# Alphas of the first two groups scanned straight from the PSUM banks, the first group in chunks of 128

## The chip, the cores and the metric

The kernel runs on one core of one Trainium2 chip. The metric is the device time of a run in microseconds (us). A core's engines each work through a queue of their own, in order: TensorE (PE in the profile; PEld its weight loads), VectorE (DVE), ScalarE (ACT), GpSimd (POOL) and SyncE (SP), which here only issues transfers. Engines wait for each other by semaphores. TensorE writes to PSUM, eight banks of 128 partitions by 512 float32 numbers.

## The reference

A gated linear attention, whose output feeds a gated state space block:

```python
# q, k, v, alpha: (4, 8, 768, 48)
for t in range(S):
    state = alpha[:, :, t, :, None] * state + np.einsum('bhd,bhe->bhde', k[:, :, t], v[:, :, t])
    y[:, :, t] = np.einsum('bhd,bhde->bhe', q[:, :, t], state)
x = y.transpose(0, 2, 1, 3).reshape(B, S, H * D)
proj = x @ w_in                      # 384 to 2 * 512
val, gate = proj[..., :512], proj[..., 512:]
for t in range(S):
    h = exp(A_log) * h + val[:, t]
    ys[:, t] = h
out = (gate * sigmoid(gate) * ys) @ w_out
```

## The kernel before

The sequence of each of the four batches is cut into three groups of 256 positions (`GC`), twelve groups in all (`m` = 0 to 11); a group has two chunks `c` of 128 positions. Attention is made chunk by chunk from scores and a carried state. For that the running product of the alphas along the sequence is needed (`prod`), and for the keys its inverse (`inv`): queries are multiplied by `prod`, keys by `inv`, both into `Z`. Two heads lie side by side on the partitions (64 each), four such pairs along the free axis, so a group's alphas are 128 x 1024 numbers.

- `products(m)` (L616) makes `prod` by one scan forwards (L629) and `inv` by one scan backwards (L641), each 1024 long and both on VectorE; small steps set the scans' starting values in `first` and `last` and note a check value in `ratio`.
- The first three groups (`NAT`) are loaded in natural order and turned by TensorE: `natural_alpha` (L572) transposes the alphas into two banks and copies them to `aT` (ScalarE L584, for chunk 1 of group 0 VectorE L586). `natural_qk` (L589) transposes keys or queries into two banks, and its `times(c)` (L603) multiplies them into `Z` on VectorE. Later groups are turned on VectorE (L620).
- `keys(m, c)` (L659) transposes the scaled keys back, ScalarE copies them (L666). `scores` (L668) makes two banks of scores; `masks` (L678) multiplies them by a triangular mask: one bank on VectorE (L687), one by a copy on ScalarE (L685) and a product on GpSimd (L686). For chunk (0, 1) both are made on VectorE (L683).
- `values`, `carried` and `state` (L689, L701, L713) make the output `y` and the state; `join` (L724) copies `y` out and places it in `xT`, partly by small transfers.
- `project`, `hidden`, `gate` and `output` (L747 to L800) are the second block; L755 is its projection, whose weights are converted from float64 bits by `high_word` (VectorE), `low_word` (ScalarE) and `word_sum` (GpSimd).

The order on each engine is the order in the text, from L814 on. First come the loads, all on SP but two on ScalarE's queue: alphas, keys and queries of group 0, alphas of group 1, values 0, keys and queries of group 1, values 1, then the weights. Then `constants` (L473), fillers for TensorE (`warm`, L827 to L831, which multiply the identity and whose result nobody uses), and the transposes. Group 0's `prod` and `inv` are made whole, then its four products into `Z`, then group 1's first scan; scores, masks, values and state of group 0 follow, then group 1's inverse, products, keys, scores and masks. From the first `project` (L907) on TensorE alternates between the two blocks.

PSUM: `ps_sc` has two banks for each of two tags (scores, `y` and, at first, keys and queries), `ps_mm` three, `ps_st` one for the state.

Of the kernel before, what the change touches and what calls it, by code (L numbers as in the profile page):

```python
# [346 lines left out]
def fast(  # L347
# [41 lines left out]
    ps_sc = pool("ps_sc", 2, space=PS)  # L389
    ps_st = pool("ps_st", 1, space=PS)  # L390
    ps_mm = pool("ps_mm", 3, space=PS)
# [76 lines left out]
    invs = inv[:, 1:].rearrange("p (h n) -> p h n", h=4)  # L468
    ratio = const.tile([C, N, 4], FP32, name="ratio")
# [6 lines left out]
    def constants():  # L476
        for m, engine in ((0, nc.vector), (1, nc.gpsimd)):
            if m:
                make_identity(nc, ident)

                nc.gpsimd.memset(mask, 1.0)
                nc.gpsimd.affine_select(out=mask, in_=mask, compare_op=ALU.is_ge, fill=0.0, base=0,
                                        channel_multiplier=-1, pattern=[[1, C]])
                for t in vs:
                    nc.gpsimd.memset(t[:, :, :, D:64], 0.0)

            for name in "akq":
                engine.memset(natural(name, m)[:, :, :, D:64], 1.0)
        for t, x in ((minus, -1.0), (start_p, FIRST_PRODUCT), (aT[:, 4 * GC:], 0.0), (first, FLOOR),
                     (last, 0.0), (one, 1.0)):  # L490
            nc.vector.memset(t, x)
        for m in range(2):
            for name in "akq":
                nc.gpsimd.memset(raw_bufs[m][name].rearrange("p h n -> p (h n)")[:, G * H * 64:], 1.0)
# [77 lines left out]
    def natural_alpha(m, banks=None):  # L572

        tps = []
        for c in range(G):
            tp = (banks or ps_mm).tile([C, 4, C], FP32, tag=f"sc{c}" if banks else "mm", name="tn")
            for p in range(4):
                nc.tensor.transpose(tp[:, p, :], natural("a", m)[:, c, 2 * p:2 * p + 2, :], ident)
            tps.append(tp)

        def evict():
            for c in range(G):
                if m or not c:
                    nc.scalar.activation(alphas[:, :, ds(c * C, C)], tps[c], AF.Copy)  # L584
                else:
                    nc.vector.tensor_copy(out=alphas[:, :, ds(c * C, C)], in_=tps[c])  # L586
        return evict

    def natural_qk(m, name, banks=None):  # L589
# [3 lines left out]
        tps = []  # L593
        for c in range(G):
            tp = (banks or ps_sc).tile([C, 4, C], FP32, tag="mm" if banks else f"sc{c}", name="tn")
            for p in range(4):
                nc.tensor.transpose(tp[:, p, :], natural(name, m)[:, c, 2 * p:2 * p + 2, :], ident)
            tps.append(tp)

        def times(c):  # L600
            i, by = {"k": (1, invs), "q": (0, prods)}[name]
            cols = ds(c * C, C)
            nc.vector.tensor_mul(Zs[m][:, :, i, cols], tps[c], by[:, :, cols])  # L603
# [12 lines left out]
    def products(m):  # L616
# [6 lines left out]
        if m >= NAT:  # L623
            check_alpha(m)
            turn("a", alphas)
        nc.vector.tensor_mul(first[:, :, 0], alphas[:, :, 0], prods[:, :, GC - 1] if g else start_p)
        nc.vector.memset(alphas[:, :, 0:1], 0.0)
        yield
        nc.vector.tensor_tensor_scan(  # L629
            out=prod, data0=aT[:, 0:4 * GC], data1=first.rearrange("p h n -> p (h n)"),  # L630
# [4 lines left out]
        if g:  # L635
            nc.vector.tensor_mul(ratio[:, m], end, inv_end)
        else:
            nc.vector.tensor_scalar(out=ratio[:, m], in0=end, scalar1=1.0 / FIRST_PRODUCT, scalar2=None,
                                    op0=ALU.mult)
        nc.vector.reciprocal(inv_end, end)  # L640
        nc.vector.tensor_tensor_scan(  # L641
            out=inv[:, ::-1], data0=aT[:, ::-1],
# [232 lines left out]
    for _ in steps:  # L875
        pass
# [153 lines left out]
```

## Time and profile before

| what | us |
|---|---|
| median of 4 runs | 296.03 (295.69 to 296.67) |
| the profiled execution | 294.53 |
| its span, from first to last instruction | 292.8 |
| busy: TensorE, VectorE, GpSimd, ScalarE | 283.3, 225.2, 112.4, 99.9 |
| landing of group 0's first alphas (issue 0.81 + 3.8) | 4.6 |
| first scores on TensorE (L675) | 15.01 |
| first projection (L755) | 30.92 |

The mean granted clock of TensorE in the profiled execution was 0.999 of full speed. A line of the timeline has the start (from the span's start), the duration, engine, source line, operation, the tile written and the tiles read, the shape, and how many instructions were merged; in square brackets how long the engine had been idle before and what ended that.

### The profile page before, as it was taken

The numbers are of one execution on the slowest core, as the hardware profiler recorded it, in microseconds if no ns is written. First come the engines' busy times: TensorE is split into PE (matmuls) and PEld (weight loads), VectorE is DVE, ScalarE is ACT, GpSimd is POOL, SyncE is SP. The second block draws the span as 40 slices with busy tenths as digits, with TensorE's granted clock in tenths as the row PEclk, the third lists the DMA queues.
The fourth block names the chain that finished last, engine by engine and source line by source line (L and its number), as shares of the span: only waits on it lengthen the run. The fifth ranks groups of instructions, "written<-read, shape, count | busy, mean of one in ns | idle before, by whom it ended". The sixth has DMA issues, their size and how long they took to land. (4 is left out here: it accounts for less than half of the span.)

```text
span 292.8 us, 6119 instructions
## 1 busy us (share of the span) xinstructions
PE 283.3 (97%) x2343; PEld 225.4 (77%) x2343; DVE 225.2 (77%) x262; ACT 99.9 (34%) x221; POOL 112.4 (38%) x114
## 2 busy tenths in 40 slices
PE   7799999999999999999999999999999999999991
PEld 3488877886886886886886896886886886886870
DVE  5997897999996898898799799799699694312211
ACT  4267534434333332323432431432441531331110
POOL 7017791374712612642612613642513542401110
PEclk9999999999999999999999999999999999999999
DMA  9999979999992991991991891991891401101101
GB/s 129 163 161 305 370 131 173 231 264 215 255 181 76 231 152 51 238 182 49 239 164 44 220 199 29 234 191 34 224 205 33 109 12 35 54 11 31 54 4 63
DMA packets 71230, 42.08 MB, mean 144 GB/s; under 512 B 47492, under 2 KB 70536, under 8 KB 71192
## 3 DMA queue, kind: packets, MB, share of 16 engines
q1 hardware_dynamic: 69760, 40.96, 68.8%
q0 software_dynamic: 384, 0.44, 0.7%
q8 instruction: 20, 0.33, 0.5%
q10 hardware_dynamic: 1048, 0.20, 0.5%
q14 instruction: 18, 0.15, 0.2%
HBM read 33.33 MB, written 4.72 MB: 130 GB/s over the span
## 5 line engine op out<-in xcount | busy, mean ns | idle before, releaser
L771 POOL TENSOR_TENSOR f<-sg,hh 128x256 f32<-128x256 f32 x48 | 60.3, 1257 | 94.7 <-ACT sg L770 44.9
L755 PE MATMUL pv<-xT,w_in 128*128 128x256 f32 x288 | 72.3, 387 | 0.0
L755 PE MATMUL pg<-xT,w_in 128*128 128x256 f32 x288 | 70.3, 380 | 0.0
L785 PE MATMUL o<-w_out,f 128*128 128x384 f32 x192 | 64.0, 486 | 0.0
L755 PEld LDWEIGHTS pg<-xT,w_in 128*128 128x128 f32 x288 | 54.5, 190 | 8.1 <-DVE hh L763 0.8
L755 PEld LDWEIGHTS pv<-xT,w_in 128*128 128x128 f32 x288 | 52.8, 190 | 10.0 <-issue 1.9
L686 POOL TENSOR_TENSOR A<-A,mask 128x512 f32<-128x512 f32 x23 | 28.8, 1271 | 67.8 <-ACT A L685 67.8
L785 PEld LDWEIGHTS o<-w_out,f 128*128 128x128 f32 x192 | 36.4, 190 | 22.6 <-POOL w_out L535 0.3
L770 ACT ACTIVATE sg<-pg 128x256 f32<-128x256 f32 x48 | 18.4, 384 | 93.6 <-PE pg L755 88.9
L763 DVE TENSOR_TENSOR_SCAN hh<-a_dec,hh,pv 128x256 f32<-128x256 f32 x32 | 23.3, 727 | 24.0 <-PE pv L755 24.0
L629 DVE TENSOR_TENSOR_SCAN prod<-aT,first 128x1024 f32<-128x1024 f32 x12 | 33.0, 2748 | 0.1
L687 DVE TENSOR_TENSOR A<-sc,mask 128x512 f32<-128x512 f32 x23 | 15.7, 690 | 20.0 <-PE sc L675 19.8
L641 DVE TENSOR_TENSOR_SCAN inv<-aT,last 128x1025 f32<-128x1025 f32 x12 | 30.0, 2504 | 0.4
L793 ACT ACTIVATE o_sb<-o 128x384 f32<-128x384 f32 x22 | 10.8, 491 | 42.7 <-PE o L785 42.7
L675 PE MATMUL sc<-Z 48*128 48x128 f32 x384 | 24.9, 279 | 0.0
L675 PEld LDWEIGHTS sc<-Z 48*128 48x128 f32 x384 | 22.4, 188 | 2.8 <-issue 1.8
L698 PE MATMUL y<-A,v 128*64 128x128 f32 x384 | 23.7, 274 | 0.2 <-POOL A L686 0.2
L698 PEld LDWEIGHTS y<-A,v 128*64 128x64 f32 x384 | 20.7, 137 | 0.8 <-POOL A L686 0.4
L620 DVE STREAM_TRANSPOSE aT<-raw_a 128x1024 f32<-128x1024 f32 x9 | 18.4, 2040 | 0.0
L620 DVE STREAM_TRANSPOSE Z<-raw_q 128x1024 f32<-128x1024 f32 x9 | 18.2, 2023 | 0.0
L620 DVE STREAM_TRANSPOSE Z<-raw_k 128x1024 f32<-128x1024 f32 x9 | 18.2, 2018 | 0.0
L719 PEld LDWEIGHTS st<-v,ktm 128*64 128x64 f32 x320 | 11.4, 137 | 3.4 <-issue 3.0
(91 smaller groups left out, 264.4 us busy)
## 6 DMA issues: line engine op xcount, KB each, us to landing
raw_k<-in_k_dram SPq DMA_DIRECT2D x24, 192.0 KB, 5.1
raw_q<-in_q_dram SPq DMA_DIRECT2D x24, 192.0 KB, 6.4
v<-in_v_dram SPq DMA_DIRECT2D x24, 192.0 KB, 6.6
out_dram<-o_sb SPq DMA_DIRECT2D x24, 192.0 KB, 1.9
raw_a<-in_alpha_dram SPq DMA_DIRECT2D x23, 192.0 KB, 3.9
raw_a<-in_alpha_dram SPq DMA_DIRECT2D x18, 176.0 KB, 4.0
raw_k<-in_k_dram SPq DMA_DIRECT2D x18, 176.0 KB, 5.9
raw_q<-in_q_dram SPq DMA_DIRECT2D x18, 176.0 KB, 6.9
```

The lines of the kernel that those rows point to most:

```text
L620: nc.vector.transpose(out=to.rearrange("p h (c j) -> p h j c", j=NT), in_=raw_bufs[m % NR][name].rearrange("p h (j d) -> p h j d", d=D)[:, ...
L629: nc.vector.tensor_tensor_scan(out=prod, data0=aT[:, 0:4 * GC], data1=first.rearrange("p h n -> p (h n)"), initial=0.0, op0=ALU.mult, op1= ...
L641: nc.vector.tensor_tensor_scan(out=inv[:, ::-1], data0=aT[:, ::-1], data1=last.rearrange("p h n -> p (h n)")[:, 0:4 * GC + 1][:, ::-1], in ...
L675: nc.tensor.matmul(sc[i][:, p, :], Z[rows, p, 1, cols], Z[rows, p, 0, cols], start=True, stop=True)
L686: nc.gpsimd.tensor_mul(A[:, 1], A[:, 1], mb)
L687: nc.vector.tensor_mul(A[:, 0], sc[0], mb)
L698: nc.tensor.matmul(ys[m][i][ds(64 * s, 64), e, ds(c * C, C)], v_sb[:, c, 2 * p + i, :], A[:, i, p, :], start=(c == 0 and e == 0), stop=Fal ...
L755: nc.tensor.matmul(pj, w_in[cc][:, kk, vg, :], xT[:, kk, :], start=(kk == 0), stop=(kk == NK - 1))
L763: nc.vector.tensor_tensor_scan(out=hh, data0=a_dec[:, cc:cc + 1].to_broadcast([C, GC]), data1=pv, initial=prev_h[cc][:, GC - 1:GC] if n % ...
L770: nc.scalar.activation(sg, pg, AF.Silu)
L771: return lambda: nc.gpsimd.tensor_mul(fs[n][:, cc, :], sg, hhs.pop((n, cc)))
L785: nc.tensor.matmul(os[c], fs[n][:, cc, ds(c * C, C)], w_out[:, cc, :], start=(cc == 0), stop=(cc == NI - 1))
```

## The change

PSUM becomes one pool `ps` with named banks: three for single tiles in turn (`mm`, "b0", "b1", "b6"), and pairs that alternate between "b4"/"b5" and one tile over two adjacent banks ("b23", `both`).

Group 0: alphas stay in their two banks, and `chunk_products` scans each chunk there, 512 at a time, with its own `first_c`, `last_c`, `prod_c` and `inv_c`. The second chunk starts from the end of the first (`ends`). Keys and queries of a chunk are multiplied, and its scores and masks begin, before the next chunk is scanned. Masks are split into `masks_far` (ScalarE and GpSimd) and `masks_near` (VectorE), for chunk (0, 1) as well.

Group 1: alphas are transposed into the two adjacent banks, and `products(1, al)` scans all 1024 from there. Of its four products into `Z`, that of the first chunk's queries is a copy on ScalarE (`q_sb`) and a product on GpSimd. The scores of both chunks stand ahead of its `keys`.

The loads of group 0 and 1 are interleaved by chunk, `first` is set first of all, seven matmuls on it take the place of the first fillers, and the later fillers are gone. ScalarE's Silu table is fetched earlier. From group 2 on the steps are the same, in the new banks.

```diff
...
-    ps_sc = pool("ps_sc", 2, space=PS)
...
-    ps_mm = pool("ps_mm", 3, space=PS)
+    ps = pool("ps", 1, space=PS)
+    next_mm, next_pair = itertools.cycle("016"), itertools.cycle((0, 1))
+    def mm(*dims, b=None):
+        return ps.tile([C, *dims], FP32, tag=f"b{b or next(next_mm)}", name="mm")
+    def pair_of(*dims, dtype=FP32):
+        if next(next_pair):
+            return [ps.tile([C, *dims], dtype, tag=f"b{b}", name="pair") for b in (4, 5)]
+        t = both()
+        n = dims[0] * dims[1]
+        return [t[:, i, 0:n].rearrange("p (x y) -> p x y", x=dims[0]).bitcast(dtype) for i in range(2)]
+    def both():
+        return ps.tile([C, 2, 4 * C], FP32, tag="b23", name="pair")
...
+    first_c = first.rearrange("p h n -> p (h n)")[:, 0:4 * C].rearrange("p (h n) -> p h n", h=4)
+    last_c = [last.rearrange("p h n -> p (h n)")[:, ds(c * 5 * C, 5 * C)].rearrange("p (h n) -> p h n", h=5)
+              for c in range(G)]
+    prod_c = [prod[:, ds(c * 4 * C, 4 * C)] for c in range(G)]
+    inv_c = [inv[:, ds(c * 4 * C, 4 * C + 1)] for c in range(G)]
...
-        for t, x in ((minus, -1.0), (start_p, FIRST_PRODUCT), (aT[:, 4 * GC:], 0.0), (first, FLOOR),
-                     (last, 0.0), (one, 1.0)):
+        nc.vector.memset(first, FLOOR)
+        make_identity(nc, ident)
+        for name in "akq":
...
+        for t, x in ((minus, -1.0), (start_p, FIRST_PRODUCT), (last, 0.0), (aT[:, 4 * GC:], 0.0), (one, 1.0)):
...
-    def natural_alpha(m, banks=None):
...
-        def evict():
-            for c in range(G):
-                if m or not c:
-                    nc.scalar.activation(alphas[:, :, ds(c * C, C)], tps[c], AF.Copy)
-                else:
-                    nc.vector.tensor_copy(out=alphas[:, :, ds(c * C, C)], in_=tps[c])
-        return evict
...
-    def natural_qk(m, name, banks=None):
+    def turned(name, m, c, tp):
+        for p in range(4):
+            nc.tensor.transpose(tp[:, p, :], natural(name, m)[:, c, 2 * p:2 * p + 2, :], ident)
...
+        def times():
             i, by = {"k": (1, invs), "q": (0, prods)}[name]
             cols = ds(c * C, C)
-            nc.vector.tensor_mul(Zs[m][:, :, i, cols], tps[c], by[:, :, cols])
+            if m < 1:
+                by = (inv_c[c][:, 1:] if name == "k" else prod_c[c]).rearrange("p (h n) -> p h n", h=4)
+            else:
+                by = by[:, :, cols]
+            nc.vector.tensor_mul(Zs[m][:, :, i, cols], tp, by)
...
+    ends = [start_p]
+    def chunk_products(c, al):
+        by_place = lambda t: t.rearrange("p (h n) -> p h n", h=4)
+        al_0, flat = by_place(al)[:, :, 0], last_c[c].rearrange("p h n -> p (h n)")[:, 0:4 * C]
+        prod, inv = prod_c[c], inv_c[c]
+        nc.vector.tensor_mul(first_c[:, :, 0], al_0, ends[-1])
+        nc.vector.memset(al_0, 0.0)
+        nc.vector.tensor_tensor_scan(out=prod, data0=al, data1=first_c.rearrange("p h n -> p (h n)"),
+                                     initial=0.0, op0=ALU.mult, op1=ALU.max)
+        yield
+        end, inv_end = by_place(prod)[:, :, C - 1], last_c[c][:, 1:5, 0]
+        ends.append(end)
+        if c:
+            nc.vector.tensor_scalar(out=ratio[:, 0], in0=end, scalar1=1.0 / FIRST_PRODUCT, scalar2=None,
+                                    op0=ALU.mult)
+        nc.vector.reciprocal(inv_end, end)
+        nc.vector.tensor_copy(out=inv[:, 4 * C:], in_=last_c[c][:, 4, 0:1])
+        nc.vector.tensor_tensor_scan(out=inv[:, 0:4 * C][:, ::-1], data0=al[:, ::-1], data1=flat[:, ::-1],
+                                     initial=last_c[c][:, 4, 0:1], op0=ALU.mult, op1=ALU.add)
+        yield
...
+        if al is None:
+            al = aT[:, 0:4 * GC]
+        al_0 = al.rearrange("p (h n) -> p h n", h=4)[:, :, 0]
+        if m == 1:
+            nc.vector.memset(first.rearrange("p h (c n) -> p (h c) n", c=2)[:, :, 0], FLOOR)
+        nc.vector.tensor_mul(first[:, :, 0], al_0, ends[-1] if m == 1 else prods[:, :, GC - 1] if g else start_p)
+        nc.vector.memset(al_0, 0.0)
         yield
         nc.vector.tensor_tensor_scan(
-            out=prod, data0=aT[:, 0:4 * GC], data1=first.rearrange("p h n -> p (h n)"),
...
-            nc.vector.tensor_mul(ratio[:, m], end, inv_end)
+            nc.vector.tensor_mul(ratio[:, m], end, last_c[1][:, 1:5, 0] if m == 1 else inv_end)
...
+        if m == 1:
+            nc.vector.memset(last.rearrange("p h (c n) -> p (h c) n", c=2)[:, :, 0], 0.0)
         nc.vector.reciprocal(inv_end, end)
-        nc.vector.tensor_tensor_scan(
-            out=inv[:, ::-1], data0=aT[:, ::-1],
-            data1=last.rearrange("p h n -> p (h n)")[:, 0:4 * GC + 1][:, ::-1],
-            initial=0.0, op0=ALU.mult, op1=ALU.add)
...
+        if m == 1:
+            nc.vector.tensor_copy(out=inv[:, 4 * GC:], in_=last[:, 4, 0:1])
+            nc.vector.tensor_tensor_scan(out=inv[:, 0:4 * GC][:, ::-1], data0=al[:, ::-1],
+                                         data1=lasts[:, 0:4 * GC][:, ::-1],
+                                         initial=last[:, 4, 0:1], op0=ALU.mult, op1=ALU.add)
...
-        tp = ps_mm.tile([C, 4, C], FP32, tag="mm", name="tp")
+        tp = mm(4, C, b=b)
...
-        sc = [ps_sc.tile([C, 4, C], FP32, tag=f"sc{i}", name=f"sc{i}") for i in range(2)]
+        sc = pair_of(4, C)
...
+        masks_far(m, c)
+        masks_near(m, c)
+    def mask_all():
+        return mask[:, None, :].to_broadcast([C, 4, C])
+    def masks_far(m, c):
         A, sc = As[m, c]
-        mb = mask[:, None, :].to_broadcast([C, 4, C])
-        if (m, c) == (0, 1):
-            for i in range(2):
-                nc.vector.tensor_mul(A[:, i], sc[i], mb)
-            return
         nc.scalar.activation(A[:, 1], sc[1], AF.Copy)
-        nc.gpsimd.tensor_mul(A[:, 1], A[:, 1], mb)
-        nc.vector.tensor_mul(A[:, 0], sc[0], mb)
+        nc.gpsimd.tensor_mul(A[:, 1], A[:, 1], mask_all())
+    def masks_near(m, c):
+        A, sc = As[m, c]
+        nc.vector.tensor_mul(A[:, 0], sc[0], mask_all())
...
-            ys[m] = [ps_sc.tile([C, 2, GC], FP32, tag=f"sc{i}", name=f"y{i}") for i in range(2)]
+            ys[m] = pair_of(2, GC) if m else [mm(2, GC, b=b) for b in "06"]
...
-        pv = ps_mm.tile([C, GC], FP32, tag="mm", name="pv")
-        pg = ps_mm.tile([C, GC], FP32, tag="mm", name="pg")
+        pv, pg = mm(GC), mm(GC)
...
-    pair("k", 0, SP, SP)
-    pair("q", 0, SP, SP)
-    pair("a", 1, SP, SP)
-    load_v(0, SP)
-    pair("k", 1, SP, SP)
-    pair("q", 1, SP, SP)
+    for c in range(G):
+        for name in "kq":
+            load_natural(name, 0, c, SP)
+    for c in range(G):
+        load_natural("a", 1, c, SP)
+        load_v(0, SP, [c])
+    for c in range(G):
+        for name in "kq":
+            load_natural(name, 1, c, SP)
...
-    def warm(count):
-        t = ps_mm.tile([C, 4, C], FP32, tag="mm", name="warm")
-        for _ in range(count):
-            nc.tensor.matmul(t, ident, ident[:, None, :].to_broadcast([C, 4, C]), start=True, stop=True)
     nc.scalar.activation(ok[:, 0:1], minus, AF.Exp)
-    warm(2)
-    evict = natural_alpha(0)
-    al = ps_mm.tile([C, NI], FP32, tag="mm", name="al")
-    nc.tensor.transpose(al, a_log, ident[0:NI, 0:NI])
-    evict()
-    nc.scalar.activation(a_dec, al, AF.Exp)
+    t = st.rearrange("p h d -> p (h d)")[:, 0:C]
+    for _ in range(7):
+        nc.tensor.matmul(t, first_c[:, 0], first_c[:, 0], start=True, stop=True)
+    als = [mm(4, C, b=b) for b in "01"]
+    for c in range(G):
+        turned("a", 0, c, als[c])
+    tl = st[:, 0, 0:NI]
+    nc.tensor.transpose(tl, a_log, ident[0:NI, 0:NI])
+    nc.scalar.activation(a_dec, tl, AF.Exp)
+    nc.scalar.activation(ok[:, 0:1], minus, AF.Silu)
     check_alpha(0)
-    k_times, q_times = natural_qk(0, "k"), natural_qk(0, "q")
-    warm(2)
-    evict = natural_alpha(1)
-    warm(2)
-    for _ in products(0):
+    qk = [natural_qk(0, name, c, tp) for c in range(G) for name, tp in zip("kq", pair_of(4, C))]
+    for _ in chunk_products(0, als[0].rearrange("p h n -> p (h n)")):
         pass
-    evict()
-    check_alpha(1)
-    steps = products(1)
+    qk[0]()
+    qk[1]()
+    scores(0, 0)
+    masks_far(0, 0)
+    keys(0, 0, "6")
+    steps = chunk_products(1, als[1].rearrange("p h n -> p (h n)"))
+    next(steps)
+    masks_near(0, 0)
+    al = both()
     for c in range(G):
-        k_times(c)
-        q_times(c)
+        turned("a", 1, c, al.rearrange("p b (h n) -> p (b h) n", n=GC)[:, :, ds(c * C, C)])
+    next(steps)
+    qk[2]()
+    qk[3]()
+    values(0, 0)
+    state(0, 0)
+    scores(0, 1)
+    masks_far(0, 1)
+    keys(0, 1, "1")
+    steps = products(1, al.rearrange("p b n -> p (b n)"))
     next(steps)
     next(steps)
-    for c in range(G):
-        scores(0, c)
-    nc.scalar.activation(ok[:, 0:1], minus, AF.Silu)
-    for c in range(G):
-        masks(0, c)
-    for c in range(G):
-        keys(0, c)
-    values(0, 0)
-    state(0, 0)
+    masks_near(0, 1)
+    k10, q10 = (ps.tile([C, 4, C], FP32, tag=f"b{b}", name="pair") for b in (4, 5))
+    natural_qk(1, "q", 0, q10)
+    q_sb = p1.tile([C, 4, C], FP32, tag="q_sb", name="q_sb")
+    nc.scalar.activation(q_sb, q10, AF.Copy)
+    nc.gpsimd.tensor_mul(Zs[1][:, :, 0, 0:C], q_sb, prods[:, :, 0:C])
+    check_alpha(1)
     values(0, 1)
     state(0, 1)
     carried(0, 1)
+    qk = [natural_qk(1, "k", 0, k10), natural_qk(1, "k", 1, mm(4, C, b="1"))]
     join(0, (SP, nc.gpsimd))
     for i in range(2, NI):
         load_w_in(i, SP)
     for i in range(2):
         load_w_out(i, SP)
-    k_times, q_times = natural_qk(1, "k"), natural_qk(1, "q", ps_mm)
-    for _ in steps:
-        pass
-    for c in range(G):
-        k_times(c)
-        q_times(c)
-    for c in range(G):
-        keys(1, c)
-        scores(1, c)
-        masks(1, c)
+    qk.append(natural_qk(1, "q", 1, mm(4, C, b="6")))
+    next(steps)
+    qk[0]()
+    next(next_pair)
+    scores(1, 0)
+    masks_far(1, 0)
+    qk[1]()
+    qk[2]()
+    masks_near(1, 0)
+    scores(1, 1)
+    masks(1, 1)
+    keys(1, 0, "1")
+    keys(1, 1, "0")
     low_word(0)
     state(1, 0)
     values(1, 0)
-    banks = [ps_sc.tile([C, 4, C], U32, tag=f"sc{i}", name=f"bank{i}") for i in range(2)]
+    banks = pair_of(4, C, dtype=U32)
...
-    natural_alpha(2, ps_sc)()
+    for c, tp in enumerate(pair_of(4, C)):
+        turned("a", 2, c, tp)
+        nc.scalar.activation(alphas[:, :, ds(c * C, C)], tp, AF.Copy)
...
-            k_times, q_times = natural_qk(m, "k"), natural_qk(m, "q")
-            for c in range(G):
-                k_times(c)
-                q_times(c)
+            for times in [natural_qk(m, name, c, tp) for c in range(G) for name, tp in zip("kq", pair_of(4, C))]:
+                times()
...
```

## The prediction

> **What bounds the kernel now.** First the page's busy line and its 40 slices:
>
> ```profile
> PE 283.3 (97%) x2343; PEld 225.4 (77%) x2343; DVE 225.2 (77%) x262; ACT 99.9 (34%) x221; POOL 112.4 (38%) x114
> ...
> PE   7799999999999999999999999999999999999991
> ```
>
> TensorE is full from the third slice to the last, and the waits of TensorE after 30 us are nil, those of its weight loads some 0.3 us or less each. So the change can only gain or lose ahead of that stretch, and what it gains there arrives at the end if TensorE's queue stays full. The chain of waits holds only the last copy and tells nothing. So I read the timeline of TensorE, whose columns are start, duration, engine, line, operation:
>
> ```profile
> 10.61 1.88 PE L831 MATMUL warm<-ident 128*128 128x512 f32 x4
> ...
> 15.01 2.06 PE L675 MATMUL sc<-Z 48*128 48x128 f32 x32
> ...
> 26.70 0.67 PE L719 MATMUL st<-v,ktm 128*64 128x48 f32 x16
> ...
> 30.92 1.56 PE L755 MATMUL pv<-xT,w_in 128*128 128x256 f32 x6
> ...
> 71.86 2.06 PE L675 MATMUL sc<-Z 48*128 48x128 f32 x32
> ```
>
> Real work is dense from 15.01; before that there are transposes as their data land, from 5.00, and fillers (L831). The first projection (L755, 30.92) is my milestone: behind it the order of work is unchanged. Ahead of it VectorE leads:
>
> ```profile
> 6.42 0.69 DVE L586 COPY aT<-tn 128x512 f32<-128x512 f32 x1 [2.23 <-ACT aT L584]
> ...
> 7.48 2.29 DVE L629 TENSOR_TENSOR_SCAN prod<-aT,first 128x1024 f32<-128x1024 f32 x1
> ...
> 14.29 0.68 DVE L603 TENSOR_TENSOR Z<-tn,prod 128x512 f32<-128x512 f32 x1
> ...
> 54.82 2.03 DVE L620 STREAM_TRANSPOSE aT<-raw_a 128x1024 f32<-128x1024 f32 x1
> ...
> 59.13 2.79 DVE L629 TENSOR_TENSOR_SCAN prod<-aT,first 128x1024 f32<-128x1024 f32 x1
> ...
> 70.42 1.23 DVE L652 TENSOR_TENSOR Z<-Z,prod 128x1024 f32<-128x1024 f32 x1
> ```
>
> From 6.42 to 25 us it hardly rests, and the first scores (15.01) follow its fourth product of queries and keys (14.29 + 0.68).
>
> **The change, part by part.**
>
> *Start.* The copy out of the bank (0.69) goes; the chain begins when chunk 0's alphas are transposed. ScalarE read that bank at 5.79 before. The fillers ahead of the transposes become 7 matmuls of 128 columns, from about 1.9 (the memset of `first`, 0.91 from 0.93) instead of 1.43. Each is two records, as in L831. The old ones took (5.00 - 1.43)/4 = 0.89 per 512 columns, so 0.22 per 128: 14 records end at 5.0, as before. From below 0.13 (a transpose's spacing), which ends at 3.7, but the alphas land only at 4.65 (0.81 plus 3.8 to landing). From above 0.34, the weight load beside the cold fillers: 6.7. I take 0.22, with colder transposes: VectorE starts at 5.95, between 5.5 and 7.3.
>
> *Scans in chunks.* A scan costs 2.29 for 1024 (L629) and about 0.7 for 256 (L763), hence 1.22 for 512; start to dependent start 1.26, and 1.33 to a product, from 2.33 and 2.40 in the rows. Other steps by start-to-start times: first multiply to scan 0.33 (7.15 to 7.48), reciprocal to what needs it 0.2, product to product 0.61. Chunk 0: multiply 5.95, scan 6.28, reciprocal 7.54, copy 7.75, scan 7.96, keys 9.29, queries 9.90 to 10.57. Scores of chunk 0 at 10.6 instead of 15.01. Chunk 1: 10.50, scan 10.83, mask of chunk 0 at 11.97 (its scores end at 11.8), reciprocal 12.64, copy 12.85, scan 13.05, products 14.38 and 14.98 to 15.66. That is only 0.7 behind the old whole group, with one mask done already.
>
> *Group 1 from two banks.* A memset and multiply at 15.6, scan 16.0, mask (0,1) 18.22, five small steps (ratio, memset, reciprocal, copy; 1.3 in all), scan 19.53, products 21.93, 22.54, 23.14 to 23.82. Gone from VectorE: one whole mask (L683, 0.64) and one of four products (0.6). The last scores start at 23.86.
>
> *The tail to the milestone.* Scores 1.03, then the eight key transposes that now follow them; ScalarE copies the second scores and then the keys (0.6 each), so the states start at 26.25 instead of 26.70. From there before took 30.92 - 26.70 = 4.22, with a 0.17 wait for GpSimd's mask, which now ends at 27.0, ahead of need: 4.05. Milestone 30.30, a gain of 0.62.
>
> *What covers the moved work.* The group-1 alphas are transposed in the middle of TensorE's queue and wait for two things: the bank pair, free after the mask at 12.65, and their load. Loads land every 1.2 us; the second half moves from the seventh to the eighth place on SP, so from 7.16 + 5.3 = 12.5 to 13.7. Behind this wait stand values, state and scores of (0,0)/(0,1): 14.2, 15.2, 15.75 to 16.8, whose first reader is the mask at 18.22: 1.4 us of cover; beyond it each microsecond is one on the path. Keys and queries interleaved by chunk land before their use (the last at 10.1); group 1's land by 19.7, needed from 20.9. ScalarE's second table load (1.28) moves from 15.16 to about 6.4, where that engine idled. GpSimd's product (row L686: 1.27) runs from about 18.9 to 20.2, needs `q_sb` (0.6 on ScalarE, 18.1 to 18.7) and the scan at 18.2, and is used at 22.6; behind it on GpSimd wait the four transfers of `join` (ready at 21.9). The `w_in` sums start at 27.7, after ScalarE's word, against 28.88. All of these are hidden. In group 2 only the order of 16 transposes differs.
>
> *Does GpSimd slow a scan?* This pair of rows shows a price; the scan has just been shown:
>
> ```profile
> 60.28 2.16 POOL L771 TENSOR_TENSOR f<-sg,hh 128x256 f32<-128x256 f32 x1 [0.51 <-ACT sg L770]
> ```
>
> A scan that otherwise takes 2.29 took 2.79 and the product 2.16 instead of 0.73. Both scan operands lay in SBUF. The scan at 37.93 read a bank and took 0.68 beside a GpSimd sum. The new scans read a bank too, so I take 0; the other end is 0.5 each for two long scans that overlap, plus 0.5 in chunk 1.
> [...]
>
> *The clock.* The fillers at 10.6 and 13.2 go. The profile shows that after 5.6 us of sparse transposes alone, the four L831 records at 10.61 took 0.43 apiece, half of the cold 0.89, so the clock had held; the new scores come after the same stretch. I take 0 for this term.
> A rule speaks against that: the Trainium skill ("TensorE: Matmul & The Clock Gate"), Part 4, says that transposes do not count as busy, and Part 1 that some 3.4 us idle halves the clock. By it the scores at 10.6 would run at half speed, and the sum would be that of rival 1. The records at 10.61 disagree.
>
> *Where the stall goes.* After the milestone VectorE's next fixed point is the load of group 3's alphas (L620, 54.82). The third of its four transfers lands at 48.15 + 5.6 = 53.7; the second landed 0.6 after the first, so the fourth at 54.35. The transfer queue ahead of it stays full but for its pause near 40 us, which the last weights' landing (28.89 + 9.4) sets. That doesn't move, so VectorE can gain only 0.4 there. Its work then runs without a gap to 71.65 (70.42 + 1.23), for scores that start at 71.86: TensorE can keep 0.4 + 0.2 = 0.6.
>
> **Sum.** 0.62 ahead, at most 0.6 kept: 0.6 off the profiled execution, whose span is 292.8 within a time of 294.5. The median of the runs is 296.03, so 295.4.
>
> **Rivals.**
> 1. *Slower: without the fillers the clock is halved when real work begins.* The first scores take 1.0 more, so the mask behind them (11.97) waits 0.95, and with it all of VectorE's chain. If the clock stays halved, transposes, values, state and scores behind the load at 13.7 take 2.1 + 2.1 + 1.0 + 2.1: the second scores end at 20.9 instead of 16.8, and the mask at 18.22 waits 2.7. Milestone 33.0, 298.1. If it returned after 3.6 us of work, as from 1.43 to 5.0, only the 0.95 would remain (296.4), so the rival needs a half clock past the first scores, and decides once that mask is more than 0.62 late. For it: gaps of half a microsecond all along. Against it: the row at 10.61.
> 2. *No change: contention or a late start eats the gain.* Three contended scans cost 1.5 and leave +0.9 (296.9) at worst; one costs 0.5 and leaves -0.1, 295.9. Slow fillers alone: start 0.4 later, -0.2, 295.8. For it: GpSimd has three products beside the scans; against it: the scans' bank operand.
> 3. *More gain.* Transposes at the landing, VectorE at 5.5: a front gain of 1.05, and the load of 54.35 lands earlier than read: 295.0. Against it: the full transfer queue.
>
> **Numbers.** The forecast has 0.55, and as 0.6 us is itself the bound of what a measurement can tell from no change (0.2%), I give 0.31 of it to faster and 0.24 to no change. Rival 1 has 0.14, rival 2 0.20 (0.11 no change, 0.09 slower), rival 3 0.11, all faster. Faster 0.42, same 0.35, slower 0.23. The range 294.9 to 296.8 takes in all but rival 1's full price, the worst contention, the slowest fillers (start at 7.3, 1.35 lost, 296.8) in part, and a tail of rival 3: no more than 0.2.
>
> **What will show it.** First scores near 10.6; 512-column scans of 1.2; VectorE's first multiply at 5.95; long scans of 2.3 from the banks beside GpSimd; L755's successor at 30.3; a VectorE wait of 0.2 before group 3's alphas. Wrong would be score records at twice 0.065, a milestone after 30.9, or a gain above 0.6 that survives 72 us.

## Result and profile after

| | median us | runs |
|---|---|---|
| the kernel before, in the same rounds | 295.82 (294.31 to 297.69) | 70 |
| changed | 295.72 (295.19 to 297.34) | 44 |

The ratio is 0.9997, with a 95% interval of 0.9987 to 1.0007: no difference that can be measured. The forecast was 295.4, a gain of 0.6 us. The profiled execution of the changed kernel took 296.1 us (span 294.4).

First the page's busy line and TensorE's 40 slices, as shown of before:

```profile
PE 281.1 (95%) x2345; PEld 226.4 (77%) x2345; DVE 225.1 (76%) x269; ACT 99.2 (34%) x220; POOL 113.5 (39%) x116
...
PE   7679999999999999999999999999999999999991
```

TensorE is again full behind the third slice; what differs lies for the most part ahead of 31 us, in its timeline:

```profile
5.20 1.65 PE L595 MATMUL mm<-ident,raw_a 128*128 128x128 f32 x8
...
10.99 1.16 PE L717 MATMUL pair<-Z 48*128 48x128 f32 x16 [0.17 <-DVE first L630]
...
27.78 0.67 PE L766 MATMUL st<-v,ktm 128*64 128x48 f32 x16 [0.31 <-ACT ktm L708]
...
31.61 10.63 PE L801 MATMUL mm<-xT,w_in 128*128 128x256 f32 x48
...
72.90 2.06 PE L717 MATMUL pair<-Z 48*128 48x128 f32 x32
```

The first scores come 4.0 us earlier than before (10.99 against 15.01), as foreseen, and at full speed (0.07 a record). Yet the first projection, the prediction's milestone, is at 31.61 instead of 30.30. VectorE's timeline shows where those 1.31 us went:

```profile
6.30 0.17 DVE L630 TENSOR_TENSOR first<-mm,start_p 128x4 f32<-128x4 f32 x1 [2.10 <-PE mm L595]
...
11.09 1.22 DVE L632 TENSOR_TENSOR_SCAN prod<-mm,first 128x512 f32<-128x512 f32 x1
12.89 0.69 DVE L734 TENSOR_TENSOR A<-pair,mask 128x512 f32<-128x512 f32 x1 [0.58 <-ACT A L729]
13.50 0.74 DVE L638 TENSOR_SCALAR ratio<-prod 128x4 f32<-128x4 f32 x1
14.15 0.17 DVE L640 RECIPROCAL last<-prod 128x4 f32<-128x4 f32 x1
...
20.89 2.34 DVE L681 TENSOR_TENSOR_SCAN inv<-pair,last 128x1024 f32<-128x1024 f32 x1
```

And GpSimd's, for the same stretches:

```profile
12.94 1.27 POOL L730 TENSOR_TENSOR A<-A,mask 128x512 f32<-128x512 f32 x1 [7.00 <-ACT A L729]
...
20.33 1.28 POOL L922 TENSOR_TENSOR Z<-q_sb,prod 128x512 f32<-128x512 f32 x1
```

Against the forecast's own times:

- The second chunk's multiply is 0.27 late (10.77 against 10.50), since the chain began at 6.30 and not 5.95; the steps between took 0.08 less than foreseen.
- The mask of chunk (0,0) should then have begun at 12.24; it begins at 12.89. The bracket says that VectorE idled 0.58 for ScalarE's copy at L729, though that copy reads the other bank. That makes 0.65.
- The small step `ratio` of chunk 1 took 0.74, where four numbers per partition take 0.17 elsewhere. It ended at 14.24, as GpSimd's mask product did (12.94 + 1.27 = 14.21). The reciprocal behind it is 1.51 late, so this made 0.59.
- The rest went a little faster than foreseen (27.78 to 31.61 is 3.83, for 4.05): 0.27 + 0.65 + 0.59 - 0.20 = 1.31.

The scans themselves were not slowed: the inverse scan took 2.34 with GpSimd's product beside it from 20.33 to 21.61, and 2.34 without it in e7 below.

### The profile page after: what moved, and what is told of

Read it like the earlier page. It is cut to its first block, busy times and chain, and to the rows that moved or that the text cites. A ratio compares the mean times of both kernels' runs of the same rounds, so it can differ in the third digit from the quotient of the medians.

```text
span 294.4 us, 6126 instructions
## 1 busy us (share of the span) xinstructions
PE 281.1 (95%) x2345; PEld 226.4 (77%) x2345; DVE 225.1 (76%) x269; ACT 99.2 (34%) x220; POOL 113.5 (39%) x116
## 5 line engine op out<-in xcount | busy, mean ns | idle before, releaser
L801 PE MATMUL mm<-xT,w_in 128*128 128x256 f32 x576 | 131.1, 384 | 0.0
L801 PEld LDWEIGHTS mm<-xT,w_in 128*128 128x128 f32 x576 | 107.3, 190 | 18.0 <-issue 2.0
L831 PE MATMUL mm<-w_out,f 128*128 128x384 f32 x192 | 64.4, 487 | 0.0
L831 PEld LDWEIGHTS mm<-w_out,f 128*128 128x128 f32 x192 | 36.2, 190 | 23.1 <-POOL w_out L555 0.6
L816 ACT ACTIVATE sg<-mm 128x256 f32<-128x256 f32 x48 | 18.4, 383 | 94.2 <-PE mm L801 92.1
L809 DVE TENSOR_TENSOR_SCAN hh<-a_dec,hh,mm 128x256 f32<-128x256 f32 x32 | 23.2, 726 | 20.2 <-PE mm L801 20.1
L717 PE MATMUL pair<-Z 48*128 48x128 f32 x384 | 25.1, 279 | 1.2 <-DVE first L660 0.9
L717 PEld LDWEIGHTS pair<-Z 48*128 48x128 f32 x384 | 22.6, 188 | 3.6 <-issue 2.1
L745 PE MATMUL pair<-A,v 128*64 128x128 f32 x352 | 21.3, 274 | 0.0
L745 PEld LDWEIGHTS pair<-A,v 128*64 128x64 f32 x352 | 19.1, 137 | 0.0
L729 ACT ACTIVATE A<-pair 128x512 f32<-128x512 f32 x24 | 13.3, 597 | 6.9 <-PE pair L717 5.6
```

Of the source, the lines that this page charges most:

```text
L717: nc.tensor.matmul(sc[i][:, p, :], Z[rows, p, 1, cols], Z[rows, p, 0, cols], start=True, stop=True)
L745: nc.tensor.matmul(ys[m][i][ds(64 * s, 64), e, ds(c * C, C)], v_sb[:, c, 2 * p + i, :], A[:, i, p, :], start=(c == 0 and e == 0), stop=Fal ...
L801: nc.tensor.matmul(pj, w_in[cc][:, kk, vg, :], xT[:, kk, :], start=(kk == 0), stop=(kk == NK - 1))
L809: nc.vector.tensor_tensor_scan(out=hh, data0=a_dec[:, cc:cc + 1].to_broadcast([C, GC]), data1=pv, initial=prev_h[cc][:, GC - 1:GC] if n % ...
L816: nc.scalar.activation(sg, pg, AF.Silu)
L831: nc.tensor.matmul(os[c], fs[n][:, cc, ds(c * C, C)], w_out[:, cc, :], start=(cc == 0), stop=(cc == NI - 1))
```

## The experiments

Every run has a profile of one execution, whose main times are below, and a ratio to the kernel before measured beside it. "Multiply" is VectorE's first multiply, "scores 0, 3" the first scores of groups 0 and 3, "end" that of the last copy of the output. Profiles of one kernel differ among themselves (rows 1 to 4), so small differences of the last columns mean little.

| | multiply | scores 0 | projection | scores 3 | end | span | ratio (95%) |
|---|---|---|---|---|---|---|---|
| before | 7.15 | 15.01 | 30.92 | 71.86 | 287.45 | 292.8 | |
| before_again | 7.76 | 14.99 | 31.52 | 72.46 | 288.06 | 294.4 | |
| changed | 6.30 | 10.99 | 31.61 | 72.90 | 288.50 | 294.4 | 0.9997 (0.9987-1.0007) |
| after_again | 5.71 | 10.71 | 31.34 | 73.57 | 289.03 | 294.3 | 0.9982 (0.9957-1.0008) |
| e1_two_tiles | 6.30 | 10.91 | 30.43 | 73.86 | 289.31 | 294.9 | 0.9972 (0.9946-0.9998) |
| e2_ratio_later | 6.30 | 11.00 | 30.97 | 72.25 | 287.85 | 293.2 | 0.9986 (0.9959-1.0014) |
| e3_both | 6.30 | 10.90 | 30.34 | 72.16 | 287.62 | 292.9 | 0.9965 (0.9937-0.9992) |
| e4_alphas_first | 6.16 | 10.83 | 30.32 | 71.54 | 287.40 | 292.5 | 0.9963 (0.9939-0.9986) |
| e5_before_alphas_first | 7.76 | 14.97 | 31.53 | 72.47 | 288.06 | 293.3 | 0.9981 (0.9963-1.0000) |
| e6_early_fillers | 5.50 | 10.78 | 30.27 | 72.02 | 287.60 | 293.0 | 0.9973 (0.9953-0.9993) |
| e7_product_on_vector | 6.30 | 10.90 | 30.94 | 71.88 | 287.76 | 293.1 | 0.9977 (0.9955-0.9999) |
| e8_scores_first | 6.10 | 10.71 | 30.19 | 71.90 | 287.56 | 292.8 | 0.9969 (0.9943-0.9995) |
| e10_no_fillers | 5.94 | 10.73 | 30.21 | 71.26 | 286.93 | 292.1 | 0.9960 (0.9938-0.9982) |
| e10_again | 5.89 | 10.68 | 30.15 | 71.09 | 286.67 | 292.4 | 0.9962 (0.9943-0.9981) |

### The two losses at the front

The changed kernel once more, as the base:

> The changed kernel once more, beside the others on one chip, to see how far a profile repeats. Both theories: mask of chunk (0,0) waits about 0.6 for ScalarE's copy (12.9 instead of 12.3), the ratio step behind it takes 0.74 instead of 0.17, first projection at 31.6 (before: 30.9). Time within 0.2% of before. If the projection moves by more than 0.3 between the two profiles, single profiles can't settle a step of 0.6.

Theory A: the mask waits for ScalarE because both banks of scores are one tile. In e1_two_tiles the near banks are two tiles of one bank each (only group 1's alphas still take both), in a pool of their own, `far`, that is released and made again around those alphas (not shown):

```diff
-        t = both()
-        n = dims[0] * dims[1]
-        return [t[:, i, 0:n].rearrange("p (x y) -> p x y", x=dims[0]).bitcast(dtype) for i in range(2)]
+        return [far.tile([C, *dims], dtype, tag=f"b{b}", name="pair") for b in (2, 3)]
```

> Banks 2 and 3 are two tiles of one bank each wherever scores, keys, queries and weight words use them; only the alphas of group 1 still have one tile over both. Theory A (one tile over two banks makes VectorE's mask wait for ScalarE's copy of the other bank): no wait before the masks of (0,0) and (1,1), mask (0,0) at 12.3; the ratio step then starts just before GpSimd's mask, not beside it, and is short again; first projection at 30.5, time 0.3 to 0.4% under before. Theory B (the ratio step is held by GpSimd whatever the tile): the mask is earlier but the ratio ends at 14.2 as now; projection 31.6, time as before.

Theory B: `ratio` is held by GpSimd's product. In e2_ratio_later it is only moved behind the inverse scan:

```diff
-        if c:
-            nc.vector.tensor_scalar(out=ratio[:, 0], in0=end, scalar1=1.0 / FIRST_PRODUCT, scalar2=None,
-                                    op0=ALU.mult)
         nc.vector.reciprocal(inv_end, end)
...
                                      initial=last_c[c][:, 4, 0:1], op0=ALU.mult, op1=ALU.add)
+        if c:
+            nc.vector.tensor_scalar(out=ratio[:, 0], in0=end, scalar1=1.0 / FIRST_PRODUCT, scalar2=None,
+                                    op0=ALU.mult)
         yield
```

> One tile over banks 2 and 3 as in the change; the ratio step of chunk 1 moved behind the inverse scan. Theory B: the step that follows the mask (reciprocal) starts at 13.5 instead of 14.15, first projection at 31.0, time 0.2% under the change. Theory A alone: the 0.6 wait before the mask stays, the reciprocal is held in the ratio's place, projection 31.6.

> Both edits. If the two losses add: mask (0,0) at 12.3, reciprocal at 12.9, projection at 30.4 and time 0.35 to 0.4% under before. If the first edit already frees the ratio: as e1_two_tiles. If the time lost lies in a late start (third theory), both leave the projection at 31.2 or later.

VectorE's timeline of e1_two_tiles at the place of the losses:

```profile
12.24 0.67 DVE L734 TENSOR_TENSOR A<-pair,mask 128x512 f32<-128x512 f32 x1
12.82 0.16 DVE L638 TENSOR_SCALAR ratio<-prod 128x4 f32<-128x4 f32 x1
12.89 0.17 DVE L640 RECIPROCAL last<-prod 128x4 f32<-128x4 f32 x1
```

and of e2_ratio_later:

```profile
12.89 0.69 DVE L734 TENSOR_TENSOR A<-pair,mask 128x512 f32<-128x512 f32 x1 [0.58 <-ACT A L729]
13.50 0.17 DVE L637 RECIPROCAL last<-prod 128x4 f32<-128x4 f32 x1
...
14.97 0.14 DVE L642 TENSOR_SCALAR ratio<-prod 128x4 f32<-128x4 f32 x1
```

Two tiles take the wait of 0.58 away with the same banks, data and engines, so it came from the tile and not from the bank. That it was not the new pool, the changed kernel shows by itself, in VectorE's and ScalarE's timelines at group 1:

```profile
25.41 0.69 DVE L734 TENSOR_TENSOR A<-pair,mask 128x512 f32<-128x512 f32 x1 [0.19 <-PE pair L717]
...
27.17 0.69 DVE L734 TENSOR_TENSOR A<-pair,mask 128x512 f32<-128x512 f32 x1 [1.06 <-ACT A L729]
```

```profile
25.43 0.60 ACT L729 ACTIVATE A<-pair 128x512 f32<-128x512 f32 x1 [1.31 <-issue]
```

The scores of chunk (1,0) are in two tiles of the old pool ("b4" and "b5"), and their mask at 25.41 ran beside ScalarE's copy. Those of chunk (1,1) are in the one tile "b23" again, and their mask waited 1.06 for ScalarE. The output `A` is one tile in both.

The mask being earlier, `ratio` there also ran ahead of GpSimd's product and took 0.16. In e2 the wait stays and `ratio` takes 0.14 in its new place. Multiplies at 6.30 in all three, the milestone fell from 31.61 to 30.43, 30.97 and 30.34. With both losses gone it is where the prediction had put it (30.30), in part by luck, since the start was still 0.35 late and the steps behind it were shorter by about as much.

In the times the single edits do not show. On one chip and in the same rounds the medians of 12 runs each were 296.04 (the changed kernel), 296.00 (e1), 296.05 (e2) and 295.32 (e3_both), and their ranges overlap.

The Trainium skill ("SBUF — State Buffer", Who interferes with whom) says that VectorE's `tensor_scalar` can enter a mode that needs the port pair shared with GpSimd, and that the later of the two then waits for the whole instruction of the other; the 0.74 against 0.14 to 0.17 agree. The step held here has 4 numbers a partition. Not every step is held: the reciprocal of the same size at 13.50 in e2_ratio_later took 0.17 beside the same product.

### Why 0.6 us at 30 us was not 0.6 us at 72

From the first projection to the scores of group 3 pass 40.94 us in both profiles of the kernel before, and in e5, e7 and e10_again too, the least that any profile shows. In the changed kernel it is 41.29, so 0.35 more was lost behind the milestone, and it was the single tile once more. TensorE's waits for the weights that GpSimd sums for `w_out`, first before and then changed (us in total, times, longest):

```profile
PEld o L785 <- POOL w_out L535: 0.3, 1, 0.3
...
PEld mm L831 <- POOL w_out L555: 0.6, 1, 0.6
```

VectorE prepares the words for these sums in two banks by turns (`banks`), which the change has put into the single tile. From the last step on one half to the first on the other it now took 0.59 from start to start (40.04 to 40.63), before 0.47 (39.10 to 39.57) and with two tiles in e3_both 0.48 (38.52 to 39.00), and GpSimd, which follows it, took longer for two sums:

```profile
39.80 2.00 POOL L535 TENSOR_TENSOR w_out<-w_out,wr 128x384 int32<-128x384 int32 x2
...
40.74 2.12 POOL L555 TENSOR_TENSOR w_out<-w_out,wr 128x384 int32<-128x384 int32 x2
```

After three such pairs the weight load at 42.91 waited 0.64 for a sum (before: 0.28). All three profiles with the single tile (changed, after_again, e2) have the 0.64, all others 0.27 or 0.28.

In e1_two_tiles and e3_both that loss is gone too, but against the first profile of before the gain at the milestone was used up by the scores of group 3 (73.86 and 72.16 against 71.86). VectorE's timeline of e3_both at the load of group 3's alphas, and TensorE's behind it:

```profile
54.97 2.07 DVE L650 STREAM_TRANSPOSE aT<-raw_a 128x1024 f32<-128x1024 f32 x1 [0.58 <-DMA raw_a<-in_alpha_dram]
57.07 0.97 DVE L661 TENSOR_TENSOR first<-aT,start_p 128x4 f32<-128x4 f32 x1
```

```profile
67.75 3.49 PE L831 MATMUL mm<-w_out,f 128*128 128x384 f32 x10 [0.50 <-DVE hh L809]
...
72.16 2.06 PE L717 MATMUL pair<-Z 48*128 48x128 f32 x32
```

VectorE waited 0.58 for the load and then met GpSimd's mask product with its first multiply (0.97 instead of 0.17), and TensorE stood 0.50 for a scan behind that. In e1_two_tiles the load came later still (its transfers were issued from 48.24, against 46.64 in e3_both; why is not shown):

```profile
56.67 2.06 DVE L650 STREAM_TRANSPOSE aT<-raw_a 128x1024 f32<-128x1024 f32 x1 [1.73 <-DMA raw_a<-in_alpha_dram]
```

The edit of e4_alphas_first, on top of e3_both, and of e5_before_alphas_first on the kernel before:

```diff
+    load_raw("a", 3, [SP])
     load_v(2, SP)
...
-    loads(3)
+    for name in "kq":
+        load_raw(name, 3, [SP])
```

> Edit: e3_both, with the four transfers of group 3's alphas issued ahead of group 2's two value transfers on SP. In e3_both VectorE idled 0.58 us at 54.97 for these alphas, and the 0.58 us that the front had gained (milestone 30.34 instead of 30.92) was gone at the scores of group 3 (72.16, 71.86 before). Theory L (the load caps the gain): no wait at the stream transpose L650, the alphas land about 2 us earlier (two value transfers of some 1.2 us each no longer ahead), the scores of group 3 start near 71.5, and the end of the span moves down by as much: some 0.6 us below e3_both's 292.9, a time near 294.0 in the profiled run and a median 0.5 to 0.6 below e3_both's. Rival M (VectorE's own work or its collisions with GpSimd cap it): the wait goes but the products behind it stretch by as much; scores of group 3 stay at 72.1 and nothing is gained. Rival V: group 2's values, now 2 us later, make TensorE wait at values (59.57 in e3_both): a wait on the load of v there, and a slower time.

> Edit: the kernel before, with the same two kinds of transfers swapped and nothing else. Control for e4_alphas_first. Before, VectorE did not wait for the alphas of group 3 (it was itself only ready at 54.82), so by theory L nothing is gained: milestone 30.9, scores of group 3 at 71.9, ratio 1.000. By rival M nothing either. If the order of loads is worth something by itself, the time falls by as much as in e4_alphas_first.

The same two places in e4_alphas_first, VectorE's and TensorE's:

```profile
54.43 2.03 DVE L650 STREAM_TRANSPOSE aT<-raw_a 128x1024 f32<-128x1024 f32 x1
56.50 0.17 DVE L661 TENSOR_TENSOR first<-aT,start_p 128x4 f32<-128x4 f32 x1
```

```profile
71.54 2.06 PE L717 MATMUL pair<-Z 48*128 48x128 f32 x32
```

Theory L holds up to here: no wait, and the scores of group 3 at 71.54, as expected (71.5); rival M falls, and rival V, since TensorE's values had no wait. But only 0.2 of the 0.62 reached the end (287.40 against 287.62): behind those scores a weight load now waited 0.3 for the transfer of `join` (`xT<-y_sb`), so the next transfer is already near. The ratios do not separate e4 from e3. In the control, the kernel before with that order of loads, nothing moved in the profile against before_again (31.53 and 31.52, 72.47 and 72.46), but its ratio, 0.9981, lies at the edge of no change: whether the order is worth something by itself stays open.

### The start, the clock and GpSimd's product

e6_early_fillers, on e4, starts eight fillers on the identity at 1.43; e8_scores_first, on e6, also puts the transposes of chunk 1's queries behind the scores of chunk 0; e10_no_fillers, on e4, has no fillers at all. The core of the three edits, in this order:

```diff
-    for _ in range(7):
-        nc.tensor.matmul(t, first_c[:, 0], first_c[:, 0], start=True, stop=True)
+    for _ in range(8):
+        nc.tensor.matmul(t, ident, ident, start=True, stop=True)
...
     scores(0, 0)
+    qk.append(natural_qk(0, "q", 1, q01))
...
-    for _ in range(7):
-        nc.tensor.matmul(t, first_c[:, 0], first_c[:, 0], start=True, stop=True)
```

> Edit: e4_alphas_first, with eight fillers on the identity (ready at 1.37) in place of seven on the memset of `first` (ready at 2.00). In four profiles of five the transposes of the first alphas (from 5.20) ran at 0.21 a piece and the first multiply started at 6.30; in after_again they ran at 0.13 and it started at 5.71. Theory C (TensorE becomes fast only some 3.6 us after its first work, at a point that varies): fillers from about 1.43 make all eight transposes fast; first multiply at 5.6 to 5.8 in the profile, milestone 29.8, 0.5 us gained at the front, and as much at the end if the load of group 3's alphas no longer caps it. Rival: the loads of the first alphas set the start (4.65 to 4.75), multiply unchanged at 6.3.

> Edit: e6_early_fillers, with the transposes of the queries of chunk 1 moved behind the scores of chunk 0 on TensorE. In e6_early_fillers VectorE's first multiply came 0.66 earlier than in e4_alphas_first (5.50 against 6.16), but the milestone only 0.05 earlier (30.27 against 30.32): the scores of chunk 0 stood on TensorE behind transposes whose load ended their wait at 10.19, and the mask then waited 0.53 for them. Theory Q (that order on TensorE eats the early start): scores of chunk 0 at about 10.1 if the first multiply is at 5.5, no wait at the mask, milestone 0.5 earlier (29.8); scores of group 3 at 71.0 to 71.5 if no load caps it first. If the clock rises late in the profiled run (first multiply at 6.3), half of that is gone. Rival: the alphas of group 1, which land near 13.7, or the products of chunk 1 hold the chain, and the milestone stays at 30.3.

> Edit: e4_alphas_first without the seven fillers; nothing else. TensorE's first work is then the transposes of the first alphas, near 4.8 to 5.0. Theory H (transposes raise and hold the clock like matmuls): the transposes of the first 2.8 to 5.7 us run at 0.21 apiece, so to 7.6 to 10.7; the first multiply is at 5.9 to 6.1; and the score records of chunk 0 at 10.8 take 0.07 to 0.14 each (0.07 if the clock has come). Rival (transposes do not count as busy, as the rule has it that the prediction weighed): the clock stays at half until the scores and the work behind them have run for some 3.6 us: score records at 0.14, 2.2 us for the sixteen pairs of records instead of 1.16, the mask of chunk 0 one us later, and the milestone at 31.3 or later.

In e6 VectorE started at 5.50, 0.66 before e4, but the milestone gained 0.05, a tenth of what was expected. Its mask shows why:

```profile
12.04 0.69 DVE L734 TENSOR_TENSOR A<-pair,mask 128x512 f32<-128x512 f32 x1 [0.53 <-PE pair L717]
```

The scores stood behind transposes whose queries landed at 10.19. In e8 that wait is gone, but in its profile the clock rose late and VectorE began at 6.10, so the worth of that order is not shown (30.19). In both, TensorE then waited for the loads of group 2 (in e6 0.28 at 44.19 and 0.16 at 51.46), and the scores of group 3 came later than in e4 (72.02 and 71.90): again the next transfers took the gain. Without fillers, TensorE's timeline is:

```profile
4.82 1.94 PE L595 MATMUL mm<-ident,raw_a 128*128 128x128 f32 x8 [4.82 <-DMA raw_a<-in_alpha_dram]
...
7.84 1.09 PE L595 MATMUL pair<-ident,raw_q 128*128 128x128 f32 x4
8.94 0.66 PE L595 MATMUL pair<-ident,raw_k 128*128 128x128 f32 x4
...
10.73 1.16 PE L717 MATMUL pair<-Z 48*128 48x128 f32 x16
```

Four transposes took 1.09 and from 8.94 on 0.66, and the scores 1.16 as ever: transposes alone brought the full clock, 4.1 us after the first of them, with nothing but transposes before. In e10_again it came 5.0 us after the first (9.81 against 4.76). So theory H holds. The rule weighed in the prediction (the Trainium skill, "TensorE: Matmul & The Clock Gate", Part 4, that transposes do not count as busy) is contradicted by these two runs, for the float32 transposes of this kernel.

In e7_product_on_vector, on e4, the queries of chunk 0 are multiplied on VectorE again:

```diff
-    natural_qk(1, "q", 0, q10)
-    q_sb = p1.tile([C, 4, C], FP32, tag="q_sb", name="q_sb")
-    nc.scalar.activation(q_sb, q10, AF.Copy)
-    nc.gpsimd.tensor_mul(Zs[1][:, :, 0, 0:C], q_sb, prods[:, :, 0:C])
+    q_times = natural_qk(1, "q", 0, q10)
...
     qk[0]()
+    q_times()
```

> Edit: e4_alphas_first, with the fourth product of group 1 (queries of chunk 0) back on VectorE, from the bank, between the first product of keys and the scores; ScalarE's copy to q_sb and GpSimd's product are gone. Theory: VectorE's chain there is gapless, so the part is worth one product, 0.6 us at the first scores of group 1; the milestone is 0.4 to 0.6 later than in e4_alphas_first and the end as much. Rival: the part is worth nothing, since GpSimd's product slows VectorE's scans beside it or the transfers of join behind it on GpSimd come later; the milestone does not move, or gets earlier.

The milestone is 30.94 against 30.32: the product on GpSimd is worth 0.62, one product of VectorE's gapless chain (0.60 against e3_both, which started at the same 6.30). At the milestone this part of the change paid in full; the ratios (0.9977 and 0.9963) do not separate the two.

### The base, and the last version once more

> The kernel before, unchanged, for a second profile of it. Its first profile (294.53 us, milestone 30.92, scores of group 3 at 71.86) lies 1.3 below the median of its runs with the change (295.82). Theory P (the first profile met an early clock and punctual loads): a second one shows the first multiply between 7.15 and 7.8 and the milestone later by the same amount (30.9 to 31.6), and where the alphas of group 3 land late, a VectorE wait at L620 as in e1_two_tiles. Rival: both are fixed by the program, and the second profile agrees with the first to 0.1 us at the milestone.

> e10_no_fillers unchanged, to settle whether it beats both kernels. If its ratio of 0.9960 (0.9938 to 0.9982) is real, it comes again within 0.994 to 0.998, below the change's 0.9997 (0.9987 to 1.0007); milestone near 30.2, scores of group 3 at 71.2 to 71.6. If it was luck of the rounds, the ratio lies at 0.999 or above.

The second profile of the kernel before has VectorE's first multiply and TensorE's first projection at:

```profile
7.76 0.17 DVE L626 TENSOR_TENSOR first<-aT,start_p 128x4 f32<-128x4 f32 x1
```

```profile
31.52 1.56 PE L755 MATMUL pv<-xT,w_in 128*128 128x256 f32 x6
```

Both are 0.6 later than in the first, because the eight transposes of the first alphas ran at 0.21 apiece instead of mostly 0.11; and 0.27 of waiting for group 3's alphas was there too, which TensorE did not feel (71.86 and 72.46 differ by the same 0.6). The rival is out. So the profile from which the sum was made had met an early clock: of like starts, the change is at 31.34 against 30.92 with an early clock and 31.61 against 31.52 with a late one, 0.1 to 0.4 behind at the milestone.

e10_again repeats the ratio of e10: 0.9962 (0.9943 to 0.9981) after 0.9960 (0.9938 to 0.9982), below the change's 0.9997 (0.9987 to 1.0007) without overlap. That version, the change with two tiles for the near banks, `ratio` behind the scan, group 3's alphas earlier and no fillers, is faster than the kernel before, by 1.1 us of 296 (0.38%). Against the change the times say less: measured again in after_again, the change had 0.9982 (0.9957 to 1.0008), which overlaps. The profiles speak for a gain there too, with the last copy ending at 286.93 and 286.67 against 288.50 and 289.03. What its single parts add to e3_both is too small for these ratios to tell.

## Why the prediction came out as it did

The forecast of 295.4 was for a gain of 0.6; there was none. The measured 295.72 lies within the stated 294.9 to 296.8, but not by the mechanism of the forecast: the gain at the milestone from which it was summed did not come. Point by point:

- *What bounds the kernel.* Right: TensorE is full behind the milestone, and the front is VectorE's chain.
- *Start at 5.95, between 5.5 and 7.3.* Within the bounds: 6.30 in the profile, 5.71 in the second. The seven fillers ended at 5.2, not 5.0, though at 0.21 a record, since they began at 2.05 and not 1.9; that is 0.20 of the 0.35. The other 0.15 are the four transposes behind them, at 0.21 apiece (1.10 from their start to VectorE's, for 0.95).
- *Scans in chunks.* Right: 1.22 and 1.27 for 512 columns, 2.29 and 2.34 for 1024.
- *Mask of chunk 0 at 11.97.* Wrong, and the first failing step: 0.65 of the delay. The change was read as putting the scores into two banks, and the mask was costed from TensorE's end alone; the two banks were one tile, and e1 shows that the mask therefore waited for ScalarE as well.
- *Chunk 1, reciprocal at 12.64.* Wrong, the second failing step: 0.59. `ratio` does not appear between mask and reciprocal in that sum. The timeline of before had its price, 0.51, beside the very GpSimd product (60.28 to 62.44) that the prediction showed for another purpose:

```profile
61.95 0.51 DVE L638 TENSOR_SCALAR ratio<-prod 128x4 f32<-128x4 f32 x1
```

- *Does GpSimd slow a scan?* The term of 0 was right for the scans, but contention was looked for in the scans only, and came in a step of 4 numbers.
- *The clock.* Right: full speed at the first scores, with the fillers gone.
- *The tail to the milestone, the moved work.* Right within 0.2 for the tail, and no wait for group 1's alphas outlasted its cover. But the sums of `w_in` were put at 27.7 and called hidden. They began at 29.19, and the pairs of sums, at 2.12 for 2.00 through the single tile, cost TensorE 0.35 at `w_out`.
- *Where the stall goes.* Right in place, wrong in size. The prediction had group 3's alphas land at 54.35 whatever the front did, with 0.4 to gain (54.82 - 54.35 is 0.47). Where VectorE waited for them, it could begin at 54.97 (e3_both), 55.77 (before_again), 56.37 (after_again) and 56.67 (e1): no fixed point, and there later than read. In e3_both nothing was kept against the first profile of before, 0.3 against the second; e4 shows that this load was the cap.
- *Rivals.* What happened is the second, no change by contention and a late start (295.8 to 296.9; measured 295.72, just under it), though by other instructions than it named. The first, a half clock, is out by e10.
- *The base.* The 30.92 of the milestone was taken as a property of the kernel; before_again has 31.52. And the 296.03 from which the 0.6 was taken was a median of 4 runs; 70 runs gave 295.82, so the forecast was for 0.4 under the base as measured.

## What to carry to other kernels

When a change puts two banks (or buffers) into one tile, list for each reader who else uses that tile: a reader of one half may be made to wait for the user of the other, and so may a writer. When GpSimd gets a product, look at every VectorE step beside it, the tiny ones too, for a step of four numbers can be held until the product ends (0.74 for 0.17 here). And a gain at the front is kept only up to the next transfer that was just in time, so move that transfer in the same change.

## What the runs showed of the hardware

- TensorE came to full speed (the granted clock in the traces) between 2.9 us (after_again: from 2.06 to 4.93) and 6.1 us (before_again: from 1.43 to 7.54) after its first instruction, at another point in each execution, and VectorE's start moved by up to 0.6 us with it. The Trainium skill ("TensorE: Matmul & The Clock Gate", Part 1) says that the window runs free of the kernel and that the point varies by 500 ns either way; these runs show a range of 3.2 us.
- No gain from fillers shows here (ratios 0.9960 and 0.9962 without, 0.9963 with them in e4): without them the start was at 5.94 and 5.89, ahead of seven of the nine profiles of changed versions with them (5.50 to 6.30), since the transposes then began when their data landed (4.76 to 4.82) and not behind the fillers (5.0 to 5.2 in all but e6).
- From the end of the last copy to the end of the span, with only the last transfers left, passed 5.1 to 6.3 us (e4 292.5 - 287.40 = 5.1, before_again 294.4 - 288.06 = 6.3). That and the clock make one profile a poor base for a forecast of 0.2%.
